# Scratch words and one-chunk visits in PSUM tiles of their own, and more products of zeros in the prologue, in a fused attention and mixture-of-experts kernel

## The chip, the cores and the metric

One core of one Trainium2 chip runs the whole program as one launch. The metric is the device time of an execution in microseconds, the median of several runs; smaller is better. The kernel before took 1780.86 us (median of 3, 1779.18 to 1781.14).

## The reference

Three layers follow each other on 4608 tokens of 512 columns, all in float32:

```python
scores = scale * np.matmul(q_c, k_c.transpose(0, 1, 2, 4, 3))   # 64x64 chunks, 8 heads
scores = scores - np.max(scores, axis=-1, keepdims=True)
attn = np.exp(scores); attn = attn / (np.sum(attn, axis=-1, keepdims=True) + 1e-09)
x = np.matmul(attn, v_c)                                        # -> 4608 x 512
h = x @ w_in                                                    # 512 -> 2048
x = (h - np.tanh(h)) @ w_out                                    # 2048 -> 512
noisy = x @ w_gate + log1p(exp(x @ w_noise)) * noise            # 8 experts, the best two per token
out = sum over the two of  weight * (maximum(x @ w1[e], 0) @ w2[e])
```

## The kernel before, in words

**Layout.** Tokens stand in 36 blocks of 128. The blocks form 11 groups (4, 3, 4, 3, 4, 3 blocks, then five groups of 3). For each group the dense layer runs 16 steps `f`, one for each 128 of the 2048 inner columns: layer 1 (12 products, `products1`, L313) writes a PSUM tile `hp`, `activate` makes `h - tanh(h)` and splits it into two halves of reduced precision (`gt`, L333 to L339), and layer 2 of the step before (`products2`, L385, 12 products for a group of 4 blocks, 9 for one of 3) adds into one accumulator per block (`acc`). After the 11 groups the experts run in the same way (8 experts of 3 groups and 8 steps).

**Slots.** The order is written out by hand: the program is recorded engine by engine as the Python code runs. `advance` records layer 1 of step `f`, then the functions of slot `2f`, then layer 2 of step `f-1`, then the functions of slot `2f+1`. So group `g` has slots `32g` to `32g+31`, and `at(h, fn)` puts a function into slot `h`. Every engine works off its own instructions in that order.

**Attention.** The four blocks of group 0 run in a prologue ahead of the slots (`s_mm`, `s_max`, `s_sub`, `u_x`, `e_sum`, `e_div`, `u_t`, `p_mm`, `p_hi`, `p_lo`): products q k, maximum, difference, exponential, sum, division (on POOL, L170, for the first seven blocks), transposes into a tile `pt`, a copy of it by ACT (L182), products with v, and the split into `xt` (ACT L196 high half, DVE L201 low half). The three blocks of group 1 run in the slots of group 0, one chunk at a time (`u_s_chunk`, `u_p_chunk`, L126 with 16 products of 64x64). All later blocks come in visits (`u_attn`): a visit holds the transposes of the block of the visit before, the products with v of the one before that, and the products q k of a new one. The list of visits stands at L977 to L983.

**Weights.** The dense weights arrive as 64-bit floats. In group 0 each of the 16 + 16 weight tiles is rescaled by ACT (`rebias`, L274), decoded by DVE (`decode`: three operations L287, L288, L290, through a scratch tile in PSUM), and split by `split_w` (ACT L296 the high half, POOL L298 the low half).

**PSUM.** There are eight banks. The pool `pp` holds `pair` (two banks) for the whole program and a ring of two banks with the tag `hp`: the tiles `hp`, `pt`, the prologue's scratch `word` and the target of the products of zeros (`warm_up`, L743) take turns in it. The pool `ep` holds two more pairs for the prologue and is closed before the slots; `acc` then takes its four banks. Through the slots `pair` serves everything else: `decode` writes its scratch word into `pair[:, 0]` (L285), the one-chunk visits write into `pair[:, 1]` (`one_bank`, L210), the visits into both, and the gate's small products into either (`misc`).

Of the kernel before, what the change touches and what calls it, by code (L numbers as in the profile page):

```python
# [9 lines left out]
F32 = mybir.dt.float32  # L10
# [3 lines left out]
U32 = mybir.dt.uint32  # L14
# [3 lines left out]
PSUM = bass.MemoryType.PSUM  # L18
# [12 lines left out]
def moe_chain_kernel(ctx: ExitStack, tc: tile.TileContext, q, k, v, w_in, w_out, wgn, noise,  # L31
                     w1, w2, out):
    nc = tc.nc
    NT = q.shape[0]
    NTOK = NT * 128
    GS = SIZES or [4, 3] * 3 + [3] * ((NT - 21) // 3)
# [12 lines left out]
    pp = ctx.enter_context(tc.tile_pool(name="pp", bufs=1, space=PSUM))  # L49
# [8 lines left out]

    pair = pp.tile([128, 2, 512], F32, name="pair")
    early = ExitStack()
    ep = early.enter_context(tc.tile_pool(name="ep", bufs=1, space=PSUM))
    pairs = [ep.tile([128, 2, 512], F32, name=f"pair{i}") for i in range(2)] + [pair]
    turn = {"pair": 0, "early": 0}
    accs = []

    def after(what, n):
        turn[what] += 1
        return (turn[what] - 1) % n  # L70

    def bank():
        return pair[:, after("pair", 2)]

    def misc(*shape):
        n = 1
# [7 lines left out]
    def blk(name, tag, bufs, dt=F32):  # L84
        return sp.tile([128, 512], dt, name=name, tag=tag, bufs=bufs)
# [14 lines left out]
    def load_q(i):  # L100
        Q[i] = spare("wa", NF1 - 2)[:, i % 2] if 2 <= i < GS[0] else blk("q", "q", 2)
        nc.sync.dma_start(Q[i], q[i])

    def load_k(i):
        K[i] = (spare("wa", NF1 - 1) if 2 <= i < GS[0] else ks)[:, i % 2]
        (nc.scalar if i < 2 else nc.sync).dma_start(K[i], k[i])

    def load_v(i):
        V[i] = spare("wb", NF1 - 2)[:, i % 2] if 2 <= i < GS[0] else blk("v", "v", 2)
        nc.sync.dma_start(V[i], v[i])  # L110
# [1 line left out]
    PS, MX, PT, PX, LO = {}, {}, {}, {}, {}  # L112

    def place_of(i, half):
        banks = pairs[after("early", 3)] if i < GS[0] else pair
        return banks[:, :, 256 * half:256 * half + 256].rearrange("p c (a t) -> p c a t", a=4)


# [1 line left out]
    def products(out, lhs, rhs, chunks=(0, 1)):  # L120
        for h in range(0, 8, 2):
            for c in chunks:
                rows = slice(64 * c, 64 * c + 64)
                for o in range(2):
                    cols = slice(64 * h + 64 * o, 64 * h + 64 * o + 64)
                    nc.tensor.matmul(out[64 * o:64 * o + 64, c, h // 2, :], lhsT=lhs[rows, cols],  # L126
                                     rhs=rhs[rows, cols], start=True, stop=True,
                                     tile_position=(64 * c, 64 * o))

    def s_mm(i):  # L130
        PS[i] = place_of(i, 1)
        products(PS[i], Q.pop(i), K.pop(i))
        if GS[0] <= i + 2 < NT:
            load_q(i + 2)
            load_k(i + 2)

    def s_max(i):
        MX[i] = sp.tile([128, 2, 4, 1], F32, name="mx", bufs=2)
        nc.vector.reduce_max(MX[i], PS[i], axis=AX.X)
# [24 lines left out]
    def e_div(i):  # L164
        e, sm = Et[i], SM.pop(i)
        nc.vector.tensor_scalar(sm, sm, 1e-9, None, op0=ALU.add)
        nc.vector.reciprocal(sm, sm)

        eng = nc.gpsimd if i < sum(GS[:2]) else nc.vector
        eng.tensor_tensor(e, e, sm.to_broadcast([128, 8, 64]), op=ALU.mult)  # L170
# [5 lines left out]
    def u_t(i):  # L176
        e = Et.pop(i).rearrange("p a t -> p (a t)")
        pt = pp.tile([128, 512], F32, name="pt", tag="hp", bufs=2)
        for a in range(0, 512, 128):
            nc.tensor.transpose(pt[:, a:a + 128], e[:, a:a + 128], ident)  # L180
        PT[i] = pts[:, i % 2]
        nc.scalar.copy(PT[i], pt)  # L182

    def p_mm(i):
        PX[i] = place_of(i, 0)
        products(PX[i], V.pop(i), PT.pop(i))
        if GS[0] <= i + 2 < NT:
            load_v(i + 2)
# [18 lines left out]


    def one_bank():
        return pair[:, 1].rearrange("p (c a t) -> p c a t", c=2, a=4)  # L210

    def u_s_chunk(i, c):
        if c == 0:
# [62 lines left out]
    def decode(raw, early=False):  # L276
        if raw.dtype == F32:
            return raw
        raw = raw.rearrange("p (m s) -> p m s", s=2)
        lo, hi = raw[:, :, 0], raw[:, :, 1]  # L280

        if early:
            part = pp.tile([128, 512], U32, name="word", tag="hp", bufs=2)
        else:
            part = pair[:, 0].bitcast(U32)  # L285
        x = blk("x", "y", 4, U32)
        nc.vector.tensor_scalar(part, lo, 29, None, op0=ALU.logical_shift_right)  # L287
        nc.vector.scalar_tensor_tensor(part, hi, 3, part, op0=ALU.logical_shift_left,  # L288
                                       op1=ALU.bitwise_or)
        nc.vector.scalar_tensor_tensor(x, hi, 0x80000000, part, op0=ALU.bitwise_and,  # L290
                                       op1=ALU.bitwise_or)
        return x.bitcast(F32)

    def split_w(x, tag, early=False):
        w = sp.tile([128, 2, 512], F32R, name=tag, bufs=16)
        nc.scalar.copy(w[:, 0, :], x)  # L296
        eng = nc.vector if tag == "wa" and not early else nc.gpsimd
        eng.tensor_tensor(w[:, 1, :], x, w[:, 0, :].bitcast(F32), op=ALU.subtract)  # L298
        return w
# [88 lines left out]

    def new_acc(s):
        if s.f == 0:  # L390
            s.grp["acc"] = [accs[0].tile([128, 512], F32, name="acc", bufs=4) for _ in s.tiles]

    def finish(s):
        if s.f == s.nf - 1:
# [345 lines left out]
    def warm_up(n):  # L740
        p = pp.tile([128, 512], F32, name="hp", bufs=2)
        for i in range(n):
            nc.tensor.matmul(p, lhsT=warm[:, 0:128], rhs=warm, start=True, stop=True)  # L743
# [131 lines left out]
    def prep_w(o, f):  # L875
        if f < NF1:
            (WI, WO)[o][f] = split_w(RW.pop((o, f)), ("wa", "wb")[o], True)
# [25 lines left out]
    u_x(1)  # L903
    warm_up(6)
    s_mm(2)
    u_t(0)
    s_max(2)
    e_sum(1)
# [12 lines left out]
    u_t(1)  # L921
    e_sum(3)
    e_div(3)
    p_mm(1)
    p_hi(1)
    u_t(2)
    p_mm(2)
    p_hi(2)
    decode_w(0, 0, True)
    u_t(3)  # L930
    p_mm(3)
    prep_w(0, 0)
    p_hi(3)
    for i in range(1, GS[0]):
# [7 lines left out]
    rebias_w(0, 2)  # L942
    rebias_w(1, 1)

    early.close()
    accs.append(ctx.enter_context(tc.tile_pool(name="ap", bufs=1, space=PSUM)))

    plans = [EVEN, ODD] if NG % 2 == 0 else [ODD, EVEN]
    g0 = plans[0][0]
# [10 lines left out]
    H1, H2 = 2 * NF1, 2 * NF2  # L960
    slots = [[] for _ in range(H1 * NG + H2 * E * 3 + 2)]

    def at(h, fn, *a):
        slots[h].append(L(fn, *a))
# [10 lines left out]


    n0 = sum(GS[:2])  # L977
    visits = [(H1 - 2, n0)]
    for g in range(1, NG - 1):
        hs = (4, 8, 14, 18, 22) if g == 1 else (5, 9, 15, 20) if GS[g + 1] > 3 else (5, 14, 20)  # L980
        for h in hs:
            n0 += 1
            visits.append((H1 * g + h, n0 if n0 < NT else None))  # L983
    flow = [None, None]
    for h, i in visits:
        at(h, u_attn, *flow, i)
# [5 lines left out]
    for g in range(NG):  # L992
        h0 = H1 * g
        at(h0, load_nz, g)
        if g > 0:
            n = GS[g - 1]
            for j in range(n):
                i = G0[g - 1] + j
# [3 lines left out]
            h = h0 + (11 if g + 1 < NG and GS[g + 1] > 3 else 9)  # L1002
# [65 lines left out]
    for gi, (e, ge, c0, nt, n) in enumerate(groups):  # L1068
        h0 = H1 * NG + H2 * gi
        if gi == 0:  # L1070
# [4 lines left out]
            h = h0 + 8 + GS[-1]  # L1075
# [18 lines left out]
    for g in range(NG):  # L1094
        grp = {}
        for f in range(NF1):
            s = step1(g, f)
# [3 lines left out]
    for gi, (e, ge, c0, nt, n) in enumerate(groups):  # L1101
        grp = {}
        for f in range(NF2):
            s = Step()
# [60 lines left out]
```

## Time and profile before

| | before |
|---|---|
| runs, median (lowest to highest) | 1780.86 us (1779.18 to 1781.14) |
| profiled execution, its own time | 1779.21 us |
| its span, first to last instruction | 1777.5 us |
| TensorE (PE) busy | 1742.4 us, 98% |
| VectorE (DVE), ScalarE (ACT), GpSimd (POOL) busy | 45%, 31%, 28% |
| mean granted clock of TensorE | 0.991 |

The span is time between the first and the last instruction of the profiled execution; about 1.7 us lie around it. Busy shares are means over stages that differ much: the prologue (about 24 us), group 0 with the decoding of the weights (to about 137 us), the other ten groups, and the experts. A wait is put down to the instruction that released it. The granted clock is a share of TensorE's full clock: 1.00 is 2.4 GHz and 0.50 is 1.2 GHz.

### The profile page before, as it was taken

The page shows a single profiled execution, that of the slowest core. Times are in us where ns is not written, and L with a number is a line of the kernel's source. Part 1 is how long each engine was busy: PE and PEld are TensorE (multiplying, and loading weights), DVE is VectorE, ACT ScalarE, POOL GpSimd, SP SyncE. Part 2 cuts the span into 40 slices and gives each one's busy share as a digit, 9 for nine tenths or more (in the row PEclk, how much of TensorE's full clock was granted, in tenths as well). Part 3 has the DMA queues.
Part 4 walks back from the last instruction along what each step waited for, and adds up shares of the span by engine and source line. Part 5 has one row for each costly group of instructions (what it writes and reads, how often), then busy time and mean ns, then how long its engine had stood idle before and what let it go on. Part 6 is the DMA issues. An engine that isn't in the chain of part 4 may idle for free. (4 is left out here: it accounts for less than half of the span.)

```text
span 1777.5 us, 28362 instructions
## 1 busy us (share of the span) xinstructions
PE 1742.4 (98%) x10774; PEld 1493.0 (84%) x10775; DVE 793.3 (45%) x2070; ACT 547.8 (31%) x1108; POOL 495.5 (28%) x752
## 2 busy tenths in 40 slices
PE   7999999999999999999999999999999999999997
PEld 4778888888888888888888888988899888988886
DVE  5875635454444545444375433433333333343321
ACT  4553322323232333333243223322233222232211
POOL 3551222131304032130343523322232232232112
PEclk7999999999999999999999999999999999999999
DMA  6546435453223222221344454433354343443212
GB/s 238 178 133 173 130 104 149 126 161 106 80 84 118 68 102 83 79 87 35 107 133 135 128 113 104 90 100 78 82 107 106 72 91 85 91 115 69 57 24 36
DMA packets 197830, 184.68 MB, mean 104 GB/s; under 512 B 80176, under 2 KB 139568, under 8 KB 197680
## 3 DMA queue, kind: packets, MB, share of 16 engines
q1 hardware_dynamic: 178064, 142.73, 26.8%
q0 software_dynamic: 19328, 39.41, 11.1%
q8 instruction: 96, 1.57, 0.4%
q10 hardware_dynamic: 288, 0.52, 0.1%
q14 instruction: 54, 0.44, 0.1%
HBM read 118.76 MB, written 63.84 MB: 103 GB/s over the span
## 5 line engine op out<-in xcount | busy, mean ns | idle before, releaser
L313 PE MATMUL hp<-xt,wa 128*128 128x384 f32 (+3 forms) x4416 | 888.7, 350 | 1.3 <-ACT xt L196 0.7
L385 PE MATMUL acc<-wb,gt 128*128 128x512 f32 (+1 forms) x3510 | 877.9, 395 | 0.8 <-ACT gt L337 0.8
L313 PEld LDWEIGHTS hp<-xt,wa 128*128 128x128 f32 x4416 | 769.7, 189 | 84.9 <-issue 2.2
L385 PEld LDWEIGHTS acc<-wb,gt 128*128 128x128 f32 (+1 forms) x3510 | 650.3, 188 | 136.3 <-ACT gt L337 1.4
L344 DVE SCALAR_TENSOR_TENSOR gt<-hp,gt 128x384 fp32r<-128x384 f32 (+2 forms) x192 | 113.5, 591 | 466.6 <-ACT gt L341 466.6
L341 ACT ACTIVATE gt<-hp 128x384 fp32r<-128x384 f32 (+2 forms) x192 | 99.6, 519 | 473.8 <-PE hp L313 429.8
L336 DVE TENSOR_TENSOR g<-hp,g 128x384 f32<-128x384 f32 (+1 forms) x176 | 103.8, 590 | 264.6 <-ACT g L333 264.4
L333 ACT ACTIVATE g<-hp 128x384 f32<-128x384 f32 (+1 forms) x176 | 91.5, 520 | 352.4 <-PE hp L313 340.6
L298 POOL TENSOR_TENSOR wb<-st,wb 128x512 fp32r<-128x512 f32 x64 | 93.3, 1458 | 324.5 <-ACT wb L296 324.5
L337 ACT CAST gt<-g 128x384 fp32r<-128x384 f32 (+1 forms) x176 | 95.4, 542 | 155.0 <-DVE g L336 142.5
L362 POOL COPY spacer<-mark 1x1 f32<-1x1 f32 x182 | 47.2, 259 | 340.8 <-DVE mark L357 276.7
L339 DVE TENSOR_TENSOR gt<-g,gt 128x384 fp32r<-128x384 f32 (+1 forms) x160 | 95.0, 594 | 96.1 <-ACT gt L337 96.1
L718 POOL DMA_INDIRECT out_dram<-o,lsa x73 | 119.4, 1635 | 56.3 <-DVE o L715 37.5
L537 POOL TENSOR_SCALAR r<-d 128x3 f32<-128x3 f32 (+1 forms) x11 | 5.1, 463 | 390.9 <-ACT d L528 390.8
L588 POOL DMA_INDIRECT xs<-yr,row x72 | 71.8, 997 | 31.3 <-issue 23.8
L258 DVE TENSOR_TENSOR xt<-xg,xt 128x512 fp32r<-128x512 f32 x80 | 54.3, 679 | 54.4 <-ACT xt L257 54.4
L257 ACT CAST xt<-xg 128x512 fp32r<-128x512 f32 x80 | 48.8, 610 | 95.2 <-DVE xg L435 95.0
L588 POOL DMA_INDIRECT lst<-pay,row x72 | 70.6, 980 | 15.6 <-issue 13.6
L435 DVE STREAM_TRANSPOSE xg<-xg 128x512 f32<-128x512 f32 x80 | 56.4, 705 | 0.9 <-DMA xg<-xs 0.9
L298 DVE TENSOR_TENSOR wa<-st,wa 128x512 fp32r<-128x512 f32 x64 | 45.2, 706 | 7.1 <-ACT wa L296 7.0
L296 ACT CAST wa<-st 128x512 fp32r<-128x512 f32 x64 | 39.2, 613 | 6.2 <-DMA st<-in_w_dram 6.2
L296 ACT CAST wb<-st 128x512 fp32r<-128x512 f32 x64 | 39.7, 620 | 0.8 <-DMA st<-in_w_dram 0.8
(188 smaller groups left out, 863.5 us busy)
## 6 DMA issues: line engine op xcount, KB each, us to landing
st<-in_w_dram SPq DMA_DIRECT2D x128, 256.0 KB, 2.9
xg<-xs SPq DMA_DIRECT2D x320, 64.0 KB, 2.1
out_dram<-zero SPq DMA_DIRECT2D x40, 256.0 KB, 4.5
x2d<-y SPq DMA_DIRECT2D x36, 256.0 KB, 2.2
z<-x2d SPq DMA_DIRECT2D x144, 64.0 KB, 2.0
yr<-x2d SPq DMA_DIRECT2D x36, 256.0 KB, 3.9
q<-in_q_dram SPq DMA_DIRECT2D x34, 256.0 KB, 4.0
v<-in_v_dram SPq DMA_DIRECT2D x34, 256.0 KB, 2.6
```

The lines of the kernel that those rows point to most:

```text
L296: nc.scalar.copy(w[:, 0, :], x)
L298: eng.tensor_tensor(w[:, 1, :], x, w[:, 0, :].bitcast(F32), op=ALU.subtract)
L313: nc.tensor.matmul(s.hp[:, :m], lhsT=w[:, a, d, :], rhs=s.xt[:, b, d, :m], start=(i == 0), stop=(i == 11))
L333: nc.scalar.activation(g, hp[:, :n], AF.Tanh)
L336: nc.vector.tensor_tensor(g, hp[:, :n], g, op=ALU.subtract)
L337: nc.scalar.copy(hi, g)
L339: eng.tensor_tensor(lo, g, hi.bitcast(F32), op=ALU.subtract)
L341: nc.scalar.activation(hi, hp[:, :n], AF.Relu)
L344: nc.vector.scalar_tensor_tensor(lo, hp[:, :n], 0.0, hi.bitcast(F32), op0=ALU.max, op1=ALU.subtract)
L385: nc.tensor.matmul(s.grp["acc"][j][:m], lhsT=s.gt[:, a, j * 128:j * 128 + m], rhs=s.B[s.f][:, b, :], start=(s.f == 0 and i == 0), stop=(s. ...
L588: s = nc.gpsimd.indirect_dma_start(out=to, out_offset=bass.IndirectOffsetOnAxis(ap=at, axis=0), in_=src, in_offset=None)
L718: a = nc.gpsimd.indirect_dma_start(out=out, out_offset=bass.IndirectOffsetOnAxis(ap=en[:m, 0:1], axis=0), in_=o[:m], in_offset=None, compu ...
```

## The change

1. `pair` leaves the pool `pp`. The prologue's pool `ep` holds three pairs, and the prologue's words of the tiles (0, 1) and (1, 0) go into the third of them.
2. When `ep` is closed (`first_step`), two pools open in its place: `ap` for the four accumulators, and `gp` with two tiles of one bank each, `word` for the decoding and `one` for the one-chunk visits. At slot 32, group 1's first, `gp` is closed and a pool `qp` with `pair` is opened (`decoded`).
3. The six visits that end in group 1 move: from slots 30, 36, 40, 46, 50, 54 to 33, 37, 41, 46, 50, 55. In group 3 the fourth visit moves from its slot 20 to 21.
4. The prologue gets 17 more products of zeros: 8 behind `s_mm(2)`, 2 ahead of each of `p_mm(1)`, `p_mm(2)`, `p_mm(3)`, 3 behind `p_mm(3)`.

The line numbers of the changed kernel are up to 15 higher (L126 is L136, L313 is L327, L743 is L757).

```diff
-    pair = pp.tile([128, 2, 512], F32, name="pair")
-    early = ExitStack()
+    early, decoding = ExitStack(), ExitStack()
     ep = early.enter_context(tc.tile_pool(name="ep", bufs=1, space=PSUM))
-    pairs = [ep.tile([128, 2, 512], F32, name=f"pair{i}") for i in range(2)] + [pair]
+    pairs = [ep.tile([128, 2, 512], F32, name=f"pair{i}") for i in range(3)]
+    pools = {}
...
+    def first_step():
+        early.close()
+        pools["acc"] = ctx.enter_context(tc.tile_pool(name="ap", bufs=1, space=PSUM))
+        pools["two"] = decoding.enter_context(tc.tile_pool(name="gp", bufs=1, space=PSUM))
+
+    def decoded():
+        decoding.close()
+        pools["two"] = ctx.enter_context(tc.tile_pool(name="qp", bufs=1, space=PSUM))
+        pools["pair"] = pools["two"].tile([128, 2, 512], F32, name="pair")
...
     def one_bank():
-        return pair[:, 1].rearrange("p (c a t) -> p c a t", c=2, a=4)
+        p = pools["two"].tile([128, 512], F32, name="one", bufs=1)
+        return p.rearrange("p (c a t) -> p c a t", c=2, a=4)
...
-            part = pair[:, 0].bitcast(U32)
+            if "two" in pools:
+                part = pools["two"].tile([128, 512], U32, name="word", bufs=1)
+            else:
+                part = pairs[2][:, 0].bitcast(U32)
...
     s_mm(2)
+    warm_up(8)
     u_t(0)
...
+    warm_up(2)
     p_mm(1)
     p_hi(1)
     u_t(2)
+    warm_up(2)
     p_mm(2)
     p_hi(2)
     decode_w(0, 0, True)
     u_t(3)
+    warm_up(2)
     p_mm(3)
+    warm_up(3)
     prep_w(0, 0)
...
-    visits = [(H1 - 2, n0)]
+    visits = []
+    at(H1, decoded)
     for g in range(1, NG - 1):
-        hs = (4, 8, 14, 18, 22) if g == 1 else (5, 9, 15, 20) if GS[g + 1] > 3 else (5, 14, 20)
+        hs = (1, 5, 9, 14, 18, 23) if g == 1 else (5, 9, 15, 21) if GS[g + 1] > 3 else (5, 14, 20)
         for h in hs:
+            visits.append((H1 * g + h, n0 if n0 < NT else None))
             n0 += 1
-            visits.append((H1 * g + h, n0 if n0 < NT else None))
```

Three places show what moves in the recorded order. First TensorE at the end of the prologue, from the fourth block's transposes on, with the semaphores that an instruction waits for (`_49` and the like are numbers of the build). Before:

```order
L180 MATMUL pt<-ident,e 128x128 [waits PE_49,Pool_49]
L180 MATMUL pt<-ident,e 128x128 x3
L126 MATMUL pair_76<-pts,wb_107 64x64 [waits DMAHW4_49,DVE_49,Activation_49]
L126 MATMUL pair_76<-pts,wb_107 64x64 x15
L313 MATMUL hp<-xt_309,wa 128x512 [waits DVE_49,Activation_49]
```

With the change:

```order
L190 MATMUL pt<-ident,e 128x128 [waits PE_49,Pool_49]
L190 MATMUL pt<-ident,e 128x128 x3
L757 LDWEIGHTS warm [waits DVE_49]
L757 MATMUL hp<-warm 128x512 [waits PE_49]
L757 LDWEIGHTS warm
L757 MATMUL hp<-warm 128x512
L136 MATMUL pair_75<-pts,wb_107 64x64 [waits DMAHW4_49,Activation_49]
L136 MATMUL pair_75<-pts,wb_107 64x64 x15
```

Two products of zeros stand between the transposes and the fourth block's products with v, and they wait for DVE: in the ring of two `hp` banks their bank is the one that `word` held, which DVE's L304 (L290 before) reads last. The three products of zeros of the diff follow behind these rows. With the added tiles in the ring, `word` itself now comes behind the third block's `pt` in the same bank, where before it came behind the second block's.

Second DVE in the first step of group 0: the activation, the decoding of weight tile (0, 2), the first chunk's maximum and difference, and the next decoding. Before:

```order
L336 TENSOR_TENSOR g<-hp,g 128x512
L357 MEMSET mark 1x1
L287 TENSOR_SCALAR pair<-wa_79 128x512
L288 SCALAR_TENSOR_TENSOR pair<-wa_79,pair 128x512
L290 SCALAR_TENSOR_TENSOR x<-wa_79,pair 128x512
L219 TENSOR_REDUCE mx<-pair 128x4
L220 TENSOR_TENSOR e<-pair,mx 128x4x64
L287 TENSOR_SCALAR pair<-wb_94 128x512
```

With the change:

```order
L350 TENSOR_TENSOR g<-hp,g 128x512
L371 MEMSET mark 1x1
L301 TENSOR_SCALAR word<-wa_79 128x512
L302 SCALAR_TENSOR_TENSOR word<-wa_79,word 128x512
L304 SCALAR_TENSOR_TENSOR x<-wa_79,word 128x512
L230 TENSOR_REDUCE mx<-one 128x4
L231 TENSOR_TENSOR e<-one,mx 128x4x64
L301 TENSOR_SCALAR word<-wb_94 128x512
```

The order is the same; the decoding and the visit no longer share a tile.

Third TensorE at the last visit of group 1. Before:

```order
L385 MATMUL acc<-wb,gt 128x512 x9
L313 MATMUL hp<-xt_874,wa 128x384 x12
L180 MATMUL pt<-ident,e 128x128 x4
L126 MATMUL pair<-pts,v 64x64 x16
L126 MATMUL pair<-ks,q 64x64 x16
L385 MATMUL acc<-wb,gt 128x512 x9
```

With the change:

```order
L327 MATMUL hp<-xt_916,wa 128x384 x12
L399 MATMUL acc<-wb,gt 128x512 x9
L190 MATMUL pt<-ident,e 128x128 x4
L136 MATMUL pair<-pts,v 64x64 x16
L136 MATMUL pair<-ks,q 64x64 x16
L327 MATMUL hp<-xt_916,wa 128x384 x12
```

The visit stands behind the step's layer 2 instead of ahead of it.

## Rows read from the trace of the kernel before

**Rows 1.** The page, part 1: busy time of each engine, its share and instructions.

```profile
PE 1742.4 (98%) x10774; PEld 1493.0 (84%) x10775; DVE 793.3 (45%) x2070; ACT 547.8 (31%) x1108; POOL 495.5 (28%) x752
```

**Rows 2.** Waits of PE, whole span: us in total, times, longest.

```profile
PE pair L126 <- DVE x L290: 12.1, 12, 4.8
...
PE pt L180 <- POOL e L170: 2.6, 1, 2.6
...
PE pt L180 <- DVE e L170: 1.6, 1, 1.6
...
PE pt L180 <- DVE g L336: 1.1, 1, 1.1
```

**Rows 3.** Waits of PE, from 50 to 140 us.

```profile
PE pair L126 <- DVE x L290: 6.6, 10, 1.0
```

**Rows 4.** Windows: length, busy us and count by engine, PE's granted clock, DMA.

```profile
12.68:29.75 17.07, 13.22 (x159) 9.71 (x152) 11.70 (x21) 9.12 (x17) 5.78 (x6) 0.50 0.94 373
...
29.75:33.16 3.41, 0.00 (x0) 0.00 (x0) 2.07 (x5) 2.36 (x5) 1.71 (x2) 1.00 0.00 0
```

**Rows 5.** Timeline of the prologue: start, us, engine, line, instruction, [idle before].

```profile
6.83 1.47 PE L743 MATMUL hp<-warm 128*128 128x512 bf16 x6
...
8.23 0.69 PE L126 MATMUL pair<-wa,wa 64*64 64x64 f32 x32
...
11.47 0.66 PE L180 MATMUL pt<-ident,e 128*128 128x128 f32 x4 [2.55 <-POOL e L170]
...
15.90 1.13 PE L126 MATMUL pair<-pts,v 64*64 64x64 f32 x32 [0.92 <-ACT pts L182]
...
16.53 0.67 DVE L287 TENSOR_SCALAR word<-wa 128x512 uint32<-128x512 uint32 x1
...
16.96 1.11 PE L180 MATMUL pt<-ident,e 128*128 128x128 f32 x4
...
17.97 0.69 DVE L290 SCALAR_TENSOR_TENSOR x<-wa,word 128x512 uint32<-128x512 uint32 x1
...
18.17 0.59 ACT L182 COPY pts<-pt 128x512 f32<-128x512 f32 x1 [0.49 <-PE pt L180]
...
21.72 1.13 PE L126 MATMUL pair<-pts,wb 64*64 64x64 f32 x32 [0.73 <-ACT pts L182]
...
23.55 5.49 PE L313 MATMUL hp<-xt,wa 128*128 128x512 f32 x12 [0.70 <-ACT xt L196]
```

**Rows 6.** Timeline of group 0's first steps.

```profile
27.98 0.69 DVE L290 SCALAR_TENSOR_TENSOR x<-wb,pair 128x512 uint32<-128x512 uint32 x1
...
33.83 1.12 PE L126 MATMUL pair<-ks,q 64*64 64x64 f32 x16 [4.79 <-DVE x L290]
...
34.88 5.38 PE L313 MATMUL hp<-xt,wa 128*128 128x512 f32 x12
...
40.09 2.97 PE L385 MATMUL acc<-wb,gt 128*128 128x512 f32 x12
...
44.41 3.06 PE L313 MATMUL hp<-xt,wa 128*128 128x512 f32 x12
```

**Rows 7.** Windows of two steps of group 0, columns as in rows 4.

```profile
51.00:58.20 7.20, 6.46 (x40) 4.97 (x40) 6.82 (x13) 3.54 (x8) 4.81 (x5) 1.00 0.26 105
...
58.20:65.40 7.20, 6.90 (x44) 5.37 (x44) 5.64 (x11) 3.85 (x8) 3.70 (x3) 1.00 0.75 247
```

**Rows 8.** Timeline of POOL and DVE in the step at 51 us.

```profile
50.86 1.28 POOL L298 TENSOR_TENSOR wb<-x,wb 128x512 fp32r<-128x512 f32 x1
...
51.59 0.58 DVE L166 TENSOR_SCALAR sm<-sm 128x8 f32<-128x8 f32 x1
```

**Rows 9.** Timeline of ACT in group 3.

```profile
370.09 0.51 ACT L337 CAST gt<-g 128x384 fp32r<-128x384 f32 x1 [4.74 <-DVE g L336]
```

**Rows 10.** Timeline of SP's queue and of DVE in group 1.

```profile
148.57 3.90 SPq L439 DMA_DIRECT2D z<-x2d  x8
...
155.04 0.70 DVE L435 STREAM_TRANSPOSE x2t<-z 128x512 f32<-128x512 f32 x1
```

More of the change, by code (lines that the diff above doesn't have):

```diff
@@ L57, in moe_chain_kernel @@
     ctx.enter_context(tc.manual_schedule())
-    pair = pp.tile([128, 2, 512], F32, name="pair")
-    early = ExitStack()
+    early, decoding = ExitStack(), ExitStack()
     ep = early.enter_context(tc.tile_pool(name="ep", bufs=1, space=PSUM))
-    pairs = [ep.tile([128, 2, 512], F32, name=f"pair{i}") for i in range(2)] + [pair]
+    pairs = [ep.tile([128, 2, 512], F32, name=f"pair{i}") for i in range(3)]
+    pools = {}
     turn = {"pair": 0, "early": 0}
-    accs = []
+    def first_step():
[6 more added lines that the diff above has]
+        pools["pair"] = pools["two"].tile([128, 2, 512], F32, name="pair")
     def after(what, n):
@@ L72, in bank @@
     def bank():
-        return pair[:, after("pair", 2)]
+        return pools["pair"][:, after("pair", 2)]
     def misc(*shape):
@@ L114, in place_of @@
     def place_of(i, half):
-        banks = pairs[after("early", 3)] if i < GS[0] else pair
+        banks = pairs[after("early", 3)] if i < GS[0] else pools["pair"]
         return banks[:, :, 256 * half:256 * half + 256].rearrange("p c (a t) -> p c a t", a=4)
@@ L390, in new_acc @@
         if s.f == 0:
-            s.grp["acc"] = [accs[0].tile([128, 512], F32, name="acc", bufs=4) for _ in s.tiles]
+            s.grp["acc"] = [pools["acc"].tile([128, 512], F32, name="acc", bufs=4) for _ in s.tiles]
     def finish(s):
@@ L943, in moe_chain_kernel @@
     rebias_w(1, 1)
-    early.close()
-    accs.append(ctx.enter_context(tc.tile_pool(name="ap", bufs=1, space=PSUM)))
+    first_step()
     plans = [EVEN, ODD] if NG % 2 == 0 else [ODD, EVEN]
```

## The prediction, made before the changed kernel ran

> **What bounds the kernel now.** I read the page first: TensorE is busy 98% of the span [rows 1], so a change can win only what TensorE idles, some 35 us, or what it does at the lower clock. Then I read the waits of TensorE over the whole span [rows 2]. The largest is not a lack of data: 12.1 us in 12 waits of the attention products (L126) for DVE's last decoding operation (L290). The two have no data in common. The products write `pair[:, 1]`, the decoding uses `pair[:, 0]`, and the wait comes from their sharing one tile. Ten of the twelve lie between 50 and 140 us, 6.6 us together [rows 3]; the longest, 4.79 us, is in the first step [rows 6].
>
> Next the windows, for the clock [rows 4]. From 12.68 to 29.75 us TensorE had the grant 0.50, that is 1.2 GHz. The full clock then came back for 3.41 us in which no matmul ran at all. The timeline shows what that costs: layer 1 of a step takes 5.49 us in the prologue and 5.38 us in the second step, against 3.06 us at full clock [rows 5, 6].
>
> A last look goes to DVE. It is off TensorE's path as a whole, but in group 0 it is nearly as full: 6.82 us of work in one step of 7.20 us, 5.64 us in the next, where TensorE has 6.46 and 6.90 us [rows 7]. So I ask of each freed wait whether DVE can keep up.
>
> **The change part by part.** The sum is made against the profiled execution, 1779.21 us. It lies 1.65 us below the median 1780.86 and at the low end of the runs shown; I add half of that, 0.8 us, at the end.
>
> *Eight products of zeros behind `s_mm(2)`.* They cost 1.47 / 6 = 0.245 us each at full clock [rows 5], together 1.96 us, from 8.92 us on, and end at about 10.9 us. The transposes behind them wait for POOL until 11.47 us anyway [rows 5]: cost nothing, 0.6 us to spare. In the rows the clock fell right after that idle stretch. I take it that it now holds.
>
> *The rest of the prologue at full clock.* Up to the products at 15.90 us nothing moves, since they wait for ACT's copy, which waits for the chain of exponentials. From there those products take 0.69 instead of 1.13 us and the transposes 0.66 instead of 1.11 us [rows 5], so ACT's copy of the third block starts 0.89 us earlier, at 17.3 us, and ends at 17.9 us. Now the ring of `hp` banks bites. The word of weight tile (0, 0) comes into the bank that this copy frees; before it could start at 16.53 us. Its three operations take 18.66 - 16.53 = 2.13 us, so it ends at 20.0 us. The two products of zeros ahead of the fourth block's products wait for it and take 0.49 us, so those products start at 20.5 us; without the wait they could have started at about 19.9 us. Before they started at 21.72 us: 1.2 us won, and 0.44 us more by their own duration. Layer 1 of step 0 then starts at about 22.0 us instead of 23.55: **-1.55 us**. The last three products of zeros (0.74 us) end about there too. The ends for this term are -2.2 us (no wait for the word) and +0.9 us (no full clock, below).
>
> *Layer 1 of step 0 at full clock:* 3.06 instead of 5.49 us, **-2.43 us**, so it ends at 25.05 us.
>
> *The first one-chunk products.* Tile `one` lies where the prologue's third pair lay, and its last reader is the decoding of (1, 0). That ended at 28.67 us, 5.12 us behind layer 1's start [rows 5, 6], and moves with the low half of `xt`, so to 27.1 us. The wait shrinks from 4.79 us to 27.1 - 25.05 = 2.07 us, **-2.72 us**. These products and layer 1 of step 1 then run at full clock: 0.44 and 5.38 - 3.06 = 2.32 us, **-2.76 us**. So layer 2 of step 0 starts at about 30.6 us instead of 40.09.
>
> *The other eleven waits for L290.* The second wait is 12.1 - 4.8 - 6.6 = 0.7 us, the ten others 6.6 us [rows 2, 3]. With tiles apart, the products wait only for the difference of the chunk before, one step back: **-7.3 us**. That holds if DVE keeps pace. Two steps together give it 6.82 + 5.64 = 12.46 us of work and TensorE 6.46 + 6.90 = 13.36 us [rows 7], so it does, with little room.
>
> *What is late next.* TensorE is now 9.5 us ahead of its old times at step 1, DVE only 1.55 us. Layer 2 of step 1 needs the low half of its weight tile, which POOL makes after the low half of `gt`, two subtractions of 1.28 us [rows 8] behind DVE's L336. I put that at **+0.9 us**, once or twice; the ends are 0 and 2 us.
>
> *Group 1.* The last visit's transposes waited 1.6 us for DVE's L170 [rows 2]. One slot later is one layer 2 later, more than 2 us: **-1.6 us**. The other moved visits keep at least four slots between them; I price them at nothing, since layer 1 and 2 of two steps cover their chains, with 0 to 3.2 us (two more such waits) as the bound.
>
> *Group 3.* There the transposes wait 1.1 us for L336 [rows 2]. Behind layer 2 they no longer stand in front, but layer 2 needs what ACT's cast makes from the same L336, 0.51 us later [rows 9]: **+0.6 us**.
>
> Sum: -1.55 - 2.43 - 2.72 - 2.76 - 7.3 + 0.9 - 1.6 + 0.6 = -16.9 us, so 1762.3, and with the 0.8 us **1763.1 us**.
>
> **The clock, weighed.** Rows 4 and 5 show the grant fall after 2.55 us without a matmul in a stretch of short products. The Trainium skill says the same and more ("TensorE: Matmul & The Clock Gate", What's actually happening): the low clock is the default, recent activity lifts it, and the watch on it runs free of the program's start. By that rule the same products of zeros may hold the clock in one run and miss it in the next, and the time would be the first rival's.
>
> **The rivals.**
> - *The clock falls in the prologue all the same.* Against it: 1.96 us of dense products stand where TensorE idled. For it: between 13.5 and 15.9 us TensorE still has little to do. Then the copy stays at 18.17 + 0.59 us, the word ends at 20.9 us, the two products of zeros (0.49 us each now) hold the fourth block's until 21.9 us, and the last three delay layer 1 to 24.5 us: +0.9 us. It takes its 5.49 us, ends at 30.0 us, and nothing waits behind it: products at 30.0 instead of 33.83 us, -3.8 us; step 1 at full clock -2.76, -7.3, +0.5, -1.0 from groups 1 and 3: -14.4 us, **1765.6 us**, or 2.3 more if step 1 is slow too.
> - *DVE becomes group 0's bound.* For it: 6.82 us of work in a step for which TensorE wants 6.46 [rows 7]. The small L166 that took 0.58 us ended with POOL's subtraction beside it, at 52.17 and 52.14 us [rows 8]. The Trainium skill has that as an exclusive port shared by DVE and POOL ("SBUF — State Buffer", Who interferes with whom); the rows agree. Against it: the lighter steps. If it does, the 6.6 us come back as waits for `gt` or weights: **1769.7 us**.
> - *Group 1 pays back.* Visits at slots 33, 37 and 41 stand four slots apart beside four DVE transposes; two of them wait 1.6 us like the one that I free: **1766.3 us**.
> - *The products stay tied to the decoding.* If separate tiles don't part them, everything after the first step keeps DVE's pace, 1.55 us earlier, and only -1.55 - 2.76 - 1.0 us remain: **1774.7 us**. Against it: the recorded order names two tiles.
> - *Slower: the rows of `z` come late.* In slot 33 SP's queue now has the q and k loads of a visit ahead of the eight `z` loads. DVE transposes the first `z` 6.47 us after the first of these issues [rows 10] and works in order, so a late `z` stops the activations and TensorE behind them. An issue takes 3.90 / 8 = 0.49 us [rows 10], so two cost 1.0 us, which that gap should hide. Only if the q load itself waited more than 20 us for its buffer would the gain be eaten: **1785 us**. The products that free it stand in the same slot.
>
> **How the numbers follow.** Forecast 50% (its own range 1760.3 to 1765.0: no new wait, no loss in group 3 and the run at the profile's level below; 1.9 us of new waits above), clock 25%, group 1 8%, DVE 10%, tied products 4%, late `z` 2%, 1% for what I don't see. The range 1760.3 to 1769.0 takes in the forecast, group 1's case and both versions of the clock's, and leaves out most of the other cases. This kernel's measurement can tell about 0.2%, 3.6 us, from no change. All cases but the last end more than that below 1780.86: faster 95%, slower 2%, and 3% for mixtures near no change.
>
> **What would show it.** Right: granted clock 1.00 through the prologue, layer 1 of step 0 in about 3.1 us from about 22 us; one wait of about 2 us at the first products on `one`, and none on L304 afterwards; a short wait of layer 2 for POOL in step 1; group 0's last step some 16 us earlier than before and no wait of 1.6 us in group 1; in group 3 a wait of 1.7 us of layer 2. Wrong: waits of 0.7 us in each step under another name (DVE bounds), layer 1 at 5.5 us (clock), or waits of transposes for L170 in group 1.

## The result, and the profile of the changed kernel

The changed kernel took 1762.05 us (median of 4 runs, 1761.61 to 1763.04), the kernel before 1780.30 us beside it (4 runs, 1779.18 to 1781.14): a ratio of 0.9899, with a 95% interval of 0.9882 to 0.9916. Measured twice more, both times on one chip, the ratio was 0.9904 (0.9888 to 0.9921) and 0.9896 (0.9878 to 0.9914).

| | before | after |
|---|---|---|
| profiled execution, its own time | 1779.21 us | 1762.41 us |
| its span | 1777.5 us | 1760.4 us |
| mean granted clock of TensorE | 0.991 | 0.997 |

The page of the changed kernel, part 1, as in [rows 1]:

```profile
PE 1739.3 (99%) x10791; PEld 1489.6 (85%) x10792; DVE 791.3 (45%) x2070; ACT 547.1 (31%) x1108; POOL 492.9 (28%) x752
```

TensorE has 17 matmuls more and is busy 3.1 us less. The waits of TensorE over the whole span (us in total, times, longest), to be held against [rows 2]:

```profile
PE acc L399 <- ACT gt L351: 2.4, 3, 1.6
PE one L136 <- issue: 2.2, 1, 2.2
...
PE hp L757 <- DVE x L304: 0.7, 1, 0.7
...
PE pt L190 <- POOL e L180: 0.5, 1, 0.5
```

The 12.1 us in twelve waits are gone, and so are the 1.6 us for DVE in group 1 and the 1.1 us in group 3; the 2.6 us for POOL in the prologue are down to 0.5. New are one wait of 2.2 us, the 0.7 us of the products of zeros, and 1.6 us for ACT's `gt`.

The windows of the changed kernel, columns as in [rows 4]:

```profile
7.18:27.65 20.47, 15.45 (x270) 9.48 (x264) 16.99 (x33) 10.10 (x18) 6.71 (x6) 1.00 1.04 401
27.65:31.07 3.42, 3.42 (x23) 2.72 (x19) 1.42 (x4) 2.66 (x6) 1.31 (x2) 0.50 0.42 170
31.07:38.85 7.78, 7.78 (x48) 6.10 (x47) 6.98 (x14) 4.23 (x8) 4.30 (x4) 1.00 0.24 70
```

The clock held through the prologue from 7.18 us on, where [rows 4] had 0.50 from 12.68 us. It fell once, later, at 27.65 us. The timeline of TensorE shows behind what (start, us, engine, line, instruction, [idle before]):

```profile
20.27 0.61 PE L757 MATMUL hp<-warm 128*128 128x512 bf16 x2 [0.71 <-DVE x L304]
...
22.21 3.06 PE L327 MATMUL hp<-xt,wa 128*128 128x512 f32 x12
27.43 0.97 PE L136 MATMUL one<-ks,q 64*64 64x64 f32 x16 [2.16 <-issue]
28.33 4.29 PE L327 MATMUL hp<-xt,wa 128*128 128x512 f32 x12
32.46 2.94 PE L399 MATMUL acc<-wb,gt 128*128 128x512 f32 x12
...
38.85 3.05 PE L399 MATMUL acc<-wb,gt 128*128 128x512 f32 x12
```

Layer 1 of step 0 starts at 22.21 us and takes 3.06 us [rows 5: 23.55 and 5.49]. The first products on `one` wait 2.16 us instead of 4.79 [rows 6], the clock falls there, and layer 1 of step 1 takes 4.29 us instead of 3.06. Layer 2 of step 0 starts at 32.46 us, before at 40.09.

From the third chunk's products to layer 1 of group 1's second step TensorE never waits. A window of that stretch before, and the one after, hold the same 541 matmuls:

```profile
51.01:145.06 94.05, 88.19 (x541) 69.50 (x541) 69.96 (x127) 49.37 (x90) 52.57 (x42) 1.00 0.41 138
```

```profile
41.82:129.19 87.37, 87.37 (x541) 69.45 (x540) 70.21 (x131) 50.70 (x92) 54.01 (x43) 1.00 0.43 150
```

After the change TensorE is busy all of the 87.37 us. DVE does the same 70 us of work in less time and is not the bound. The busy time itself is 0.82 us shorter. The window of before holds nine waits, so each cost about 0.09 us beside its idle time. In the rows a group without a wait starts some 0.07 us ahead of the end that the profile gives the group before it (34.88 against 33.83 + 1.12 us in [rows 6]); behind a wait that overlap is missing.

The windows end where the second layer 1 of group 1 starts, before and after:

```profile
145.06 2.27 PE L313 MATMUL hp<-xt,wa 128*128 128x384 f32 x12
```

```profile
129.19 2.35 PE L327 MATMUL hp<-xt,wa 128*128 128x384 f32 x12
```

In group 1 no transposes wait for DVE. In group 3 (timeline of TensorE; before, 1.09 us on the transposes for L336):

```profile
352.79 2.37 PE L399 MATMUL acc<-wb,gt 128*128 128x512 f32 x9 [1.64 <-ACT gt L351]
```

### The profile page after: what moved, and what is told of

Its sections match the earlier page's. It is cut to its first block, busy times and chain, and to the rows that moved or that the text cites. A ratio compares the mean times of both kernels' runs of the same rounds, so it can differ in the third digit from the quotient of the medians.

```text
span 1760.4 us, 28384 instructions
## 1 busy us (share of the span) xinstructions
PE 1739.3 (99%) x10791; PEld 1489.6 (85%) x10792; DVE 791.3 (45%) x2070; ACT 547.1 (31%) x1108; POOL 492.9 (28%) x752
## 5 line engine op out<-in xcount | busy, mean ns | idle before, releaser
L327 PE MATMUL hp<-xt,wa 128*128 128x384 f32 (+3 forms) x4416 | 885.5, 349 | 0.6 <-DVE g L350 0.6
L327 PEld LDWEIGHTS hp<-xt,wa 128*128 128x128 f32 x4416 | 766.9, 188 | 83.6 <-issue 2.2
L350 DVE TENSOR_TENSOR g<-hp,g 128x384 f32<-128x384 f32 (+1 forms) x176 | 103.8, 590 | 257.7 <-ACT g L347 235.4
L347 ACT ACTIVATE g<-hp 128x384 f32<-128x384 f32 (+1 forms) x176 | 91.5, 520 | 335.2 <-PE hp L327 303.3
L602 POOL DMA_INDIRECT lst<-pay,row x72 | 70.1, 974 | 16.7 <-issue 15.6
```

The source lines that it names most:

```text
L327: nc.tensor.matmul(s.hp[:, :m], lhsT=w[:, a, d, :], rhs=s.xt[:, b, d, :m], start=(i == 0), stop=(i == 11))
L347: nc.scalar.activation(g, hp[:, :n], AF.Tanh)
L350: nc.vector.tensor_tensor(g, hp[:, :n], g, op=ALU.subtract)
L602: s = nc.gpsimd.indirect_dma_start(out=to, out_offset=bass.IndirectOffsetOnAxis(ap=at, axis=0), in_=src, in_offset=None)
```

## The experiments

The theory: the gain is three things. The decoding and the visits no longer meet in one tile (waits of 0.7 us a step), the prologue runs at full clock and so starts group 0 earlier, and group 1's wait is gone. Its rivals: the zeros alone bring much of it; DVE is the bound and takes it back; the first wait of 2.16 us and the clock that falls behind it hide more.

### The parts alone

**tiles_only**: the new tiles and pools, without the 17 products of zeros and with the visits in their old slots.

```diff
-    warm_up(8)
...
-    warm_up(2)
...
-    warm_up(3)
...
-    visits = []
-    at(H1, decoded)
+    visits = [(H1 - 2, n0)]
+    at(H1 - 2, decoded)
...
-        hs = (1, 5, 9, 14, 18, 23) if g == 1 else (5, 9, 15, 21) if GS[g + 1] > 3 else (5, 14, 20)
+        hs = (4, 8, 14, 18, 22) if g == 1 else (5, 9, 15, 20) if GS[g + 1] > 3 else (5, 14, 20)
...
```

> The change without its 17 products of zeros and with the visits at their old slots; only the tiles are parted. Theory (parting the tiles carries nearly all, the prologue's clock hardly matters by itself): layer 1 of step 0 takes 5.5 us as before and ends at about 29.0 us, the first products follow it within 0.3 us because the decoding of (1, 0) has ended by then, the clock is back for step 1, no wait for L304 in the later steps; layer 2 of step 0 starts at about 33.2 us instead of 40.09. Time 14.2 us below before: about 1766 us (1764.5 to 1768). Rival (the terms of the sum stand side by side, so that the zeros own the 1.55 + 2.43 + 2.76 us that were put to the clock): about 10 us below before, 1770.3 us. The waits of 1.6 us in group 1 and 1.1 us in group 3 are back in both.

It took 1765.54 us (1764.82 to 1767.22), beside 1779.75 of before on the same chip: ratio 0.9923 (0.9907 to 0.9940), 14.2 us less. The timeline of TensorE:

```profile
22.52 5.49 PE L327 MATMUL hp<-xt,wa 128*128 128x512 f32 x12 [0.70 <-ACT xt L206]
27.93 0.73 PE L136 MATMUL one<-ks,q 64*64 64x64 f32 x16
28.59 3.07 PE L327 MATMUL hp<-xt,wa 128*128 128x512 f32 x12
31.50 2.96 PE L399 MATMUL acc<-wb,gt 128*128 128x512 f32 x12
...
40.01 2.13 PE L399 MATMUL acc<-wb,gt 128*128 128x512 f32 x8 [0.89 <-POOL wb L312]
```

Layer 1 of step 0 is slow again, but nothing waits behind it: the tile `one` is free when it ends. So the tiles carry most of the gain, without the zeros. Both kernels keep the decoding's word and the visits' products in banks of their own (`pair` was two banks), so what parted them is the tile and not the bank. The wait stands in the program: before, TensorE's products on `pair` were made to wait for the decoding's last operation; with the change, those on `one` wait only for the difference (L231) of the chunk before, and the first of all for the prologue's words (below).

**zeros_only**: the kernel before with the 17 products of zeros at the same places.

```diff
     s_mm(2)
+    warm_up(8)
...
+    warm_up(2)
     p_mm(1)
...
     p_mm(3)
+    warm_up(3)
...
```

> The kernel before with the 17 products of zeros and nothing else. Theory: layer 1 of step 0 takes 3.06 us from about 22.2 us on, but the first one-chunk products still wait for the decoding of (0, 2), which comes only about 1.4 us earlier than before; so that wait grows from 4.8 to about 7 us, the clock falls in it, and layer 1 of step 1 takes 5.4 us again. Time 1.4 us below before: about 1779 us (1777.5 to 1780). Rival (the clock's terms come by themselves): 6.7 us below before, 1773.6 us.

1777.76 us (10 runs, 1776.39 to 1778.71): ratio 0.9988 (0.9979 to 0.9998), 2.0 us less. The waits and the timeline of TensorE:

```profile
PE pair L126 <- DVE x L290: 14.6, 12, 7.2
```

```profile
21.94 3.06 PE L313 MATMUL hp<-xt,wa 128*128 128x512 f32 x12
32.22 1.12 PE L126 MATMUL pair<-ks,q 64*64 64x64 f32 x16 [7.21 <-DVE x L290]
33.27 4.66 PE L313 MATMUL hp<-xt,wa 128*128 128x512 f32 x12
```

The 2.43 us that layer 1 of step 0 saves come back whole in the wait behind it, which grows from 4.79 to 7.21 us. What stays is the earlier start of step 0 (21.94 against 23.55 us) and 0.7 us of layer 1 of step 1, which takes 4.66 us where [rows 6] has 5.38.

**old_visits**: the tiles and the zeros, with the visits in their old slots.

```diff
-    visits = []
-    at(H1, decoded)
+    visits = [(H1 - 2, n0)]
+    at(H1 - 2, decoded)
...
-        hs = (1, 5, 9, 14, 18, 23) if g == 1 else (5, 9, 15, 21) if GS[g + 1] > 3 else (5, 14, 20)
+        hs = (4, 8, 14, 18, 22) if g == 1 else (5, 9, 15, 20) if GS[g + 1] > 3 else (5, 14, 20)
...
```

> The changed kernel with the visits at their old slots (30, 36, 40, 46, 50, 54, and 20 in group 3) and the pair opened at slot 30. Theory: in group 1 the wait of 1.6 us of the last visit's transposes for L180 is back, in group 3 the wait of 1.64 us of layer 2 becomes one of 1.1 us of the transposes, nothing else differs: 1.0 us more, about 1763 us. Rival (the visit taken out of group 0 gave DVE room there, or the visits in slots 33 to 41 cost something): other waits between 100 and 150 us differ, and the time moves by more than 2 us either way.

1762.91 us (1762.47 to 1764.20) beside 1778.62 of before on that chip: ratio 0.9910 (0.9894 to 0.9927), 15.7 us less, where the changed kernel had 17.2 to 18.3 in its three measurements. The intervals overlap, so by time the slots are not shown. The waits of TensorE are plain:

```profile
PE pt L190 <- DVE e L180: 1.6, 1, 1.6
...
PE pt L190 <- DVE g L350: 1.1, 1, 1.1
```

Both old waits are back, and the 1.64 us of group 3 is gone. The parts add up: 14.2 and 2.0 make 16.2, against 15.7 for both together; the slots' rows make it 1.0 more.

### Is DVE near to being the bound?

One operation of about 0.7 us more in the decoding of each layer-1 weight tile (the second operation is done twice, which changes no value), in the changed kernel (**after_more_dve**) and in the kernel before (**before_more_dve**):

```diff
...
+        if not early and which == 0:
+            nc.vector.scalar_tensor_tensor(part, hi, 3, part, op0=ALU.logical_shift_left,
+                                           op1=ALU.bitwise_or)
...
```

> The changed kernel with one decoding operation (L302, 0.7 us) of every layer 1 weight tile done twice, which leaves the values as they are: DVE has 0.73 us more in each of 14 steps of group 0. Theory (DVE keeps pace with little room: 12.46 us of work in two steps for which TensorE has 13.36): two steps then hold 13.9 us of DVE work, 0.25 us a step more than TensorE's, so 2.7 us more in all, about 1764.8 us (1763 to 1767), with short waits of TensorE for gt or for weights. Rival one (DVE has room): 0, 1762 us. Rival two (TensorE still waits for each decoding): 0.73 us in each of 12 to 14 steps, about 9 us, 1771 us.

1764.79 us (1764.60 to 1765.01), ratio 0.9916 (0.9900 to 0.9933). The changed kernel had 1762.05 to 1763.06 in its three measurements, so ten more microseconds of DVE work cost about 2 to 3. The intervals overlap, so the rows must decide: from layer 1 of step 0 to the second layer 1 of group 1 it is 109.12 us (22.01 to 131.13), where the changed kernel has 106.98 (22.21 to 129.19), 2.1 us more. The first wait on `one` grew from 2.16 to 2.89 us. The waits of TensorE from 30 to 135 us:

```profile
PE acc L402 <- POOL wb L315: 0.9, 1, 0.9
PE hp L330 <- DVE mark L374: 0.6, 2, 0.3
PE acc L402 <- ACT wb L313: 0.2, 1, 0.2
```

The first of these also stands in executions of the changed kernel and its variants in which the clock held (below). DVE takes the extra work with two waits of 0.3 us: it has room, but little more than that.

> The kernel before with the same doubled operation. Theory (in each of the 12 steps with a one-chunk visit TensorE waits for the end of the decoding through the shared tile): each wait grows by 0.73 us, 8.8 us in all, about 1789 us (1787 to 1791). Rival (the waits come from DVE's load and not from the shared tile, so both kernels suffer alike): the same 2.7 us as in the changed kernel or less, 1783 us.

1796.44 us (1795.73 to 1796.81), ratio 1.0093 (1.0076 to 1.0110): 16.7 us more, nearly twice what the theory gave. The waits:

```profile
PE pair L126 <- DVE x L293: 21.4, 12, 6.2
```

They grow by 9.3 us, near the 8.8 expected. The rest is the clock. The first of five windows with 0.50 in group 0, and TensorE's timeline around it:

```profile
45.45:48.87 3.42, 3.42 (x10) 2.65 (x9) 2.22 (x4) 0.00 (x0) 0.51 (x1) 0.50 0.78 236
```

```profile
43.98 0.68 PE L126 MATMUL pair<-ks,q 64*64 64x64 f32 x16 [1.48 <-DVE x L293]
44.59 4.60 PE L316 MATMUL hp<-xt,wa 128*128 128x512 f32 x12
...
54.08 3.06 PE L316 MATMUL hp<-xt,wa 128*128 128x512 f32 x12
```

In five steps layer 1 took 4.60 to 4.62 us instead of 3.06, 7.7 us together. With 9.3 that is 17.0. So waits twice as long (1.04 to 1.69 us, where [rows 3] has 0.66 on average) cost more than twice. The same operation costs 16.7 us with the shared tile and 2 to 3 us with tiles apart.

### What do the first wait and the fallen clock cost?

**after_again** and **after_third** are the changed kernel once more, beside the kernels below.

> The changed kernel once more, as the yardstick on this chip for the three runs beside it: 18 us below before, about 1762 us. A second trace also tells whether the clock's low stretch at step 1 stays where it was or moves with the run.

1763.06 us (1762.13 to 1764.11); the clock fell again, at 28.17 us, and layer 1 of step 1 took 4.54 us.

**no_two_zeros**: without the two products of zeros ahead of `p_mm(3)`, which wait 0.71 us for DVE.

```diff
     u_t(3)
-    warm_up(2)
     p_mm(3)
```

> The changed kernel without the two products of zeros ahead of the fourth block's products. Theory (these two wait for the word of weight tile (0, 0) and hold everything behind them): the wait of 0.7 us for L304 and the 0.5 us of the two are gone from the prologue, layer 1 of step 0 starts about 0.6 us earlier, at 21.6 us, and DVE's chain with it; 0.6 us less, about 1761.5 us. Rival (they hold the clock): the clock falls before step 0 and layer 1 of it takes up to 5.5 us; 0 to 2 us more.

1762.78 us (1762.72 to 1763.33), ratio 0.9901 (0.9885 to 0.9918); 0.3 us under after_again, which tells nothing. The timeline of TensorE:

```profile
21.44 3.06 PE L327 MATMUL hp<-xt,wa 128*128 128x512 f32 x12
26.66 1.12 PE L136 MATMUL one<-ks,q 64*64 64x64 f32 x16 [2.16 <-issue]
27.71 5.49 PE L327 MATMUL hp<-xt,wa 128*128 128x512 f32 x12
```

From the second block's products to layer 1 it is 5.42 us where the changed kernel has 5.95 (16.26 to 22.21), so 0.53 us are won as expected; then the clock is low through all of layer 1 of step 1. That the missing zeros made it fall is not shown: both_and_slot20 lacks them too, and there this layer 1 took 3.04 us.

**one_free**: the prologue's words of (0, 1) and (1, 0) in the first pair instead of the third, so that they don't lie where `one` lies.

```diff
-                part = pairs[2][:, 0].bitcast(U32)
+                part = pairs[0][:, 0].bitcast(U32)
```

> The changed kernel with the prologue's words of (0, 1) and (1, 0) in the first pair instead of the third, so that the tile of the one-chunk visits has no late reader under it. Theory (behind the wait of 2.2 us stands the chain over DVE, ACT and POOL, so most of it only moves): that wait is gone, the products start right behind layer 1 of step 0 at about 25.2 us and layer 1 of step 1 at about 25.9 us at full clock, then layer 2 of step 0 waits for gt until about 31 us instead of starting at 32.5 us, and layer 2 of step 1 waits about 1 us for POOL; 0.5 us less in all (0 to 1.5 us), about 1761.5 us. Rival (the wait and the clock behind it are worth their length): 2.2 + 1.5 us less, 1758.4 us.

1762.06 us (1761.69 to 1762.48), ratio 0.9898 (0.9882 to 0.9915), 1.0 under after_again. But the wait that the edit was to remove stayed (timeline of TensorE, and of DVE ahead of it):

```profile
26.50 0.68 PE L136 MATMUL one<-ks,q 64*64 64x64 f32 x16 [2.15 <-issue]
27.11 3.05 PE L327 MATMUL hp<-xt,wa 128*128 128x512 f32 x12
```

```profile
25.71 0.69 DVE L304 SCALAR_TENSOR_TENSOR x<-wb,pair 128x512 uint32<-128x512 uint32 x1
```

The products start 0.1 us behind L304's end, wherever the word lies, so the theory fell. The program says the same: `one` lies in the second bank of the third pair, and yet ahead of its first product TensorE is made to wait for the L304 that reads the word in the first pair. In this execution the clock did not fall.

**both_and_slot20** has both edits, and group 3's fourth visit back in slot 20.

> The changed kernel without the two products of zeros, with the words in the first pair, and with the fourth visit of group 3 back in slot 20. Theory: the three gains add, 0.6 for the chain, 0.5 for the products and 0.6 for group 3, where the wait of 1.64 us of layer 2 becomes one of 1.1 us of the transposes: 1.5 us less, about 1760.5 us (1759.5 to 1761.5). Rival (only what lies on DVE's chain counts, and group 3's wait is one and the same): 0.6 us less, 1761.4 us.

1763.26 us (1761.06 to 1764.33), ratio 0.9906 (0.9890 to 0.9923): not less than after_again's 1763.06, so by time the expectation fell. Its profiled execution shows two of the three parts: from the second block's products to layer 1 it is again 5.43 us (15.82 to 21.25), and group 3 waits 1.09 us ahead of its transposes instead of 1.64. The third, the wait on `one`, is still 2.15 us.

**own_words**: the two words go into SBUF, into the decoding's own result tile, so that DVE reads nothing of the closed pool that late.

```diff
-                part = pairs[2][:, 0].bitcast(U32)
-        x = blk("x", "y", 4, U32)
+                part = None
+        x = blk("x", "y", 4, U32); part = x if part is None else part
```

**own_words_slot20**: the same with group 3's fourth visit in slot 20.

after_third, own_words and own_words_slot20 were measured beside each other; their expectations in that order:

> The changed kernel once more, so that the two beside it stand on the same chip: 1762 to 1763 us, a wait of about 2.2 us of the first products on tile one in group 0, right behind DVE's L304 of weight tile (1, 0).

> The decodings of (0, 1) and (1, 0) work in their own result tile in SBUF, so no word lies in the pool that is closed. Theory (the wait of 2.2 us is for the last reader in the closed pool, and only the words keep that pool busy so late): the first products on one start right behind layer 1 of step 0, the wait is gone, the clock keeps 1.00 through step 1, layer 1 of step 1 takes 3.06 us; TensorE is then 2 us ahead of DVE and POOL, and about 1 us of it comes back as waits of layer 2 of step 1 for POOL: 1761 to 1762 us, 1 us less than the changed kernel beside it. Rival (the whole 2 us come back in step 1, since the weights and gt of step 1 set the pace): within 0.4 us of the changed kernel, with waits of 2 us or more for POOL or gt in steps 0 to 2. Rival (the tile waits for something else of the prologue): the wait of 2.2 us stays.

> The same, and the fourth visit of group 3 is back in its slot 20. Theory: the 1.64 us wait of layer 2 in group 3 becomes one of 1.1 us of the transposes, 0.5 us less than own_words: 1760.5 to 1761.5 us, the best of the three. By time alone 0.5 us can hardly be told; the waits in group 3 decide. Rival: no less than own_words.

| | median (lowest to highest) | ratio (95%) |
|---|---|---|
| after_third | 1762.14 (1761.64 to 1762.93) | 0.9896 (0.9878 to 0.9914) |
| own_words | 1762.65 (1761.67 to 1763.63) | 0.9900 (0.9882 to 0.9918) |
| own_words_slot20 | 1761.17 (1760.38 to 1762.87) | 0.9890 (0.9872 to 0.9908) |

TensorE in after_third, and then in own_words:

```profile
26.38 0.68 PE L136 MATMUL one<-ks,q 64*64 64x64 f32 x16 [2.15 <-issue]
26.99 3.05 PE L327 MATMUL hp<-xt,wa 128*128 128x512 f32 x12
29.97 3.04 PE L399 MATMUL acc<-wb,gt 128*128 128x512 f32 x12
...
38.66 2.14 PE L399 MATMUL acc<-wb,gt 128*128 128x512 f32 x8 [0.90 <-POOL wb L312]
```

```profile
22.04 3.05 PE L327 MATMUL hp<-xt,wa 128*128 128x512 f32 x12
25.02 0.68 PE L136 MATMUL one<-ks,q 64*64 64x64 f32 x16
25.63 3.05 PE L327 MATMUL hp<-xt,wa 128*128 128x512 f32 x12
31.07 3.07 PE L399 MATMUL acc<-wb,gt 128*128 128x512 f32 x12 [2.40 <-ACT gt L351]
...
39.37 2.13 PE L399 MATMUL acc<-wb,gt 128*128 128x512 f32 x8 [0.70 <-POOL wb L312]
```

The theory was right on the wait and the rival on the time. With the words out of PSUM the wait on `one` is gone: it was for the late readers in the closed pool. But all of it comes back at layer 2 of step 0, as 2.40 us for `gt`. ACT's timeline in own_words shows what `gt` waits for:

```profile
27.43 0.62 ACT L310 CAST wb<-x 128x512 fp32r<-128x512 f32 x1 [2.21 <-DVE x L304]
...
29.05 0.60 ACT L347 ACTIVATE g<-hp 128x512 f32<-128x512 f32 x1
30.41 0.62 ACT L351 CAST gt<-g 128x512 fp32r<-128x512 f32 x1 [0.76 <-DVE mark L371]
```

The activation of step 0 (L347) has its `hp` since 25.1 us, but it stands in ACT's queue behind the split of weight tile (1, 0) and two rescalings, and that split waits for the same L304 on DVE. So here the decoding sets the start of group 0 by ACT's order, with or without the tile. own_words could not bring it forward either: its last L304 takes 1.66 us and ends at 27.39 us, as late as the changed kernel's (27.33 us). What own_words would gain with an L304 of 0.69 us, no run shows.

How little TensorE's own state matters there, from layer 1 of step 0 to the products of the fourth chunk (from the starts in each kernel's timeline):

| | layer 1 of steps 0 and 1, us | waits on `one` / `gt` / `wb` | from step 0 to the fourth chunk |
|---|---|---|---|
| before | 5.49 and 5.38 | 4.79, then 0.73, 0.76, 0.75 for L290 | 58.22 - 23.55 = 34.67 us |
| after | 3.06 and 4.29 | 2.16 / 0 / 0 | 48.22 - 22.21 = 26.01 |
| after_third | 3.06 and 3.05 | 2.15 / 0 / 0.90 | 47.10 - 21.17 = 25.93 |
| tiles_only | 5.49 and 3.07 | 0 / 0 / 0.89 | 48.48 - 22.52 = 25.96 |
| own_words | 3.05 and 3.05 | 0 / 2.40 / 0.70 | 47.80 - 22.04 = 25.76 |
| no_two_zeros | 3.06 and 5.49 | 2.16 / 0 / 0 | 48.87 - 21.44 = 27.43 |

A slow layer 1 of step 0, the first wait, 1.2 us lost to the clock: each is paid back elsewhere within 0.3 us. after_again, old_visits, one_free, both_and_slot20 and own_words_slot20 have 25.94 to 26.26 us. Only a step 1 wholly at 0.50 costs, 1.4 us, seen once.

In own_words_slot20 group 3's transposes wait 1.1 us for L350 again, and the 1.64 us of layer 2 is gone, as expected. Its median is the lowest of all, 1.0 us under after_third, and its interval covers that of the changed kernel: a better version is not shown.

## Why the prediction held, step by step

The forecast was 1763.1 us, and the main mechanism is the one named: the shared tile. The sum for the profiled execution was -16.9 us, and -16.8 was measured (1779.21 to 1762.41). That the two agree to 0.1 us is luck. Up to the fourth chunk's products the sum has 10.8 us (1.55, 2.43, 2.72, 2.76 and the three waits of 0.73 to 0.76, less 0.9) and the rows have 10.0 (58.22 to 48.22); from there to group 1's second layer 1 it has 5.1 and the rows 5.9 (15.87 less 10.0). The 0.8 us added for the median found no counterpart: the changed kernel's profiled execution lies above its median (1762.41 and 1762.05). Term by term:

- **Start of step 0, -1.55:** 1.34 us earlier. The wait of the two products of zeros for `word`'s last reader is there, 0.71 us. But the prologue comes sooner or later by up to 1 us from one execution to the next: the three profiled executions of the changed kernel start layer 1 at 22.21, 21.20 and 21.17 us. Counted from the first transposes, which wait for POOL in [rows 5], it is 12.08 us before, 11.83 in tiles_only, and 10.31 to 10.37 in these three and zeros_only, so 1.5 to 1.8 us are the zeros'.
- **Layer 1 of step 0, -2.43, and the wait behind it, -2.72:** 2.43 and 2.63. Both sizes are right, but they are one gain: tiles_only has neither the full clock nor the wait and reaches the fourth chunk in 25.96 us all the same, and zeros_only has the full clock and gets the whole 2.43 back as wait. The parted tiles alone win the 4.79 us of the wait, so the full clock's own share of the 5.06 us (2.43 and 2.63) is 0.3 us.
- **Who holds `one`:** the prediction gave the place, "its last reader is the decoding of (1, 0)". one_free shows that the place is not it: the wait is for the late readers in the closed pool. The time came out right (2.16 for 2.07 us), since in the changed kernel the reader is the same.
- **Products and layer 1 of step 1, -2.76:** this is the term that was mis-sized. It took the clock as held. It fell at 27.65 us: 0.97 and 4.29 us instead of 1.12 and 5.38, only 1.24 us won. In after_third, where it held, the term is 2.77.
- **Layer 2 of step 1 waits for POOL, +0.9:** none listed in that execution, 0.90 in after_third. The two terms are alternatives, which the prediction had not seen: TensorE late by the clock finds the weight ready. So either way it is 25.9 to 26.0 us from step 0 to the fourth chunk, and in these two executions the fallen clock cost under 0.1 us.
- **The other eleven waits, -7.3:** 7.3 us of idle time are gone, and some 0.1 us for each wait beside it, which the sum didn't have (0.8 us behind the fourth chunk).
- **Group 1, -1.6, and group 3, +0.6:** the wait of 1.6 us is gone; in group 3 1.64 stands for 1.09. old_visits shows both the other way round.

Added up by rows: 15.87 us at group 1's second layer 1 (145.06 to 129.19), 1.6 more, less 0.55, makes 16.9.

Of the rivals, the clock that falls in the prologue did not come in any of the three profiled executions of the changed kernel. In all eleven profiled executions that have the products of zeros, the variants' among them, the grant was 1.00 from 8 to 22 us. In those three it fell later, at 27.65, at 28.17 and in one not at all. The Trainium skill ("TensorE: Matmul & The Clock Gate", What's actually happening) says that the watch on the activity runs free of the program's start; that the same kernel falls in one execution and not in the next agrees. DVE as the bound is refuted twice: 70.21 us of work in a stretch of 87.37, and after_more_dve, where ten more microseconds of it cost 2.1. Group 1 paid nothing back. The tiles did part the work, and `z` did not come late: no wait in group 1 is longer than 0.6 us.

## What to carry to other kernels

Where two engines wait for each other over data that they don't share, look for the tile or the pool that they do share; here a tile for each use took eleven of the twelve waits away, and made the kernel far less sensitive to extra work (16.7 against some 2 to 3 us). Before a first wait or a slow stretch is priced, look for the second chain that ends at the same place: here, with the activation behind a weight's split in ACT's queue, the full clock of step 0 (2.43 us), the first wait (2.16 us) and the clock of step 1 (1.2 us) moved the fourth chunk, counted from step 0, by 0.3 us at most. Gains under 0.1% were read from rows here, since the times can't tell them.

## What the runs showed of the hardware that was not expected

- **The clock fell again and again in steps with short waits.** In before_more_dve, behind the first step, eleven steps of group 0 have one wait of 1.04 to 1.69 us each. The grant fell to 0.50 (1.2 GHz) five times, each time behind a wait of 1.47 or 1.48 us, and layer 1 took 4.6 instead of 3.06 us. Behind three other waits of 1.48 to 1.69 us and behind the three of 1.04 to 1.06 us it stayed, so the length of the wait alone does not decide. With waits of 0.31 to 0.98 us in the kernel before it stayed at 1.00 from 44 to 137 us.
- **The first tile `one` of the new PSUM pool waited for the closed pool's last readers,** not for those of its own place (one_free and own_words). This is a wait that the program was built with, and not one of the chip.
- **DVE and POOL stretched each other where DVE read two operands from SBUF.** In own_words the last decoding operation has both inputs there. For weight tile (0, 1) it ran while POOL was idle; for (1, 0) it ran beside POOL's subtraction. DVE's two rows, then POOL's:

```profile
23.87 0.69 DVE L304 SCALAR_TENSOR_TENSOR x<-wa,x 128x512 uint32<-128x512 uint32 x1
...
25.73 1.66 DVE L304 SCALAR_TENSOR_TENSOR x<-wb,x 128x512 uint32<-128x512 uint32 x1
```

```profile
25.29 1.55 POOL L312 TENSOR_TENSOR wa<-x,wa 128x512 fp32r<-128x512 f32 x1 [3.25 <-ACT wa L310]
```

In the changed kernel, with the word in PSUM, the same operation took 0.69 us beside POOL's subtraction (26.64 us in its trace), and that took 1.27. The Trainium skill ("SBUF — State Buffer", Who interferes with whom) says that a DVE instruction with two inputs in SBUF contends with a GpSimd instruction that reads SBUF; the rows agree.
